# Transposes three tiles behind their scores instead of two, head 0's hash bits in a pair of score banks, and the identity loaded after head 0's queries

## The chip, the cores and the metric

The kernel runs on one core of a Trainium2 chip. The metric is device microseconds (us) for one launch, as the median of several runs. Below, PE is TensorE (matmuls), DVE is VectorE, ACT is ScalarE, POOL is GpSimd and SP is SyncE, whose queue issues nearly all transfers (DMAs). Times written as "at 16.19" are us from the start of the profiled execution.

## The reference

The program is hashed (LSH) attention followed by two layers of a gated feed-forward network. q, k and v have 2 batches, 8 heads, 768 positions and 64 channels, so there are 16 heads in all.

```python
q_bits = (einsum('bhsd,dk->bhsk', q, proj) > 0)   # 6 hash bits for each position
k_bits = (einsum('bhsd,dk->bhsk', k, proj) > 0)
mask   = bucket(q_bits)[:, :, :, None] == bucket(k_bits)[:, :, None, :]
scores = where(mask, q @ k.T / sqrt(D), -1e9)
attn   = exp(scores - max(scores));  attn = attn / (sum(attn) + 1e-9)
x = (attn @ v) laid out as (1536 rows, 512)
x = leaky(x @ w_in1) @ w_out1                     # 512 -> 2048 -> 512
x = (P(h) / (Q(h) + 1e-6)) @ w_out2, h = x @ w_in2   # 512 -> 2048 -> 512
```

## The kernel before

A head is worked in six tiles of 128 query rows. Each tile passes through four steps:

- **Scores** (`rows`, kinds `first`, `second`, `scores`): four PE matmuls of 384 columns write a pair of PSUM banks, two with the high parts of q and k (L559, from `qh` and `kx`) and two with the low parts (L564, from `ql` and `k2`). Twelve rows of `ql` and `k2` hold the hash bits, so that L564 also adds the mask's penalty.
- **Clamp** on DVE (L574) reads the pair of banks into an SBUF tile `x`, and **exp** on ACT (L580) works in place.
- **Transpose** (`flip`: "flip" and "turn" are the code's names): six PE matmuls of 128 columns with the identity `idf` (L606) write another pair of banks, named `t`. A copy, kind `take`, on ACT (L429) or DVE (L433), brings it to `pt`.
- When all six tiles of a head are copied, `mix` multiplies them by v: 24 PE matmuls (L649, `pv`) in two halves of 12.

Scores and transposes share three pairs of banks in turn (`bank_pair`, tag `s`). So a transpose has to wait until the clamp has emptied the pair used three turns before, and scores wait until a `take` has emptied theirs. `late` is the list of tiles whose transposes are still to come; `wait(2)` leaves two of them behind the scores.

For each head, `kT` and `qT` (128 x 768 floats, 0.393 MB each, tiles `rk` and `rq`) are loaded, and `k2`, `qh`, `kx` and `ql` are made from them. The hash bits come from PE matmuls against the projection (L480, tile `pb`). Head 0 and head 1 use their own `rk` and `rq`; from then on one set of matmuls serves two heads and has loads of its own, `kN` and `qN` (L472). For head 0, DVE writes the bits straight into `ql` and `k2` (`bits_at`, L489, four operations). For the others DVE writes a tile `bt` (L485), and four small DMAs (L496) carry its rows into `ql` and `k2`.

While PE is in attention, DVE and ACT also split the 64 weight blocks (`raw`, L319 and on) into high and low parts. After head 14 the matrix stages begin: 24 units of 96 PE matmuls of 512 columns (L679, L695, L698).

Every step is a task with durations per engine; `Plan.order` builds a list schedule from them, and the kernel issues its instructions in that order. `FAVOUR` gives each kind of task a bias to its rank and factors on its cost per engine. So a change of this table or of one task moves instructions everywhere.

Of the kernel before, what the change touches and what calls it, by code (L numbers as in the profile page):

```python
# [61 lines left out]
WARMUP = 9  # L62

PORT = ("dve", "pool")
FAVOUR = {
    "a_abs": (62.5, {}), "a_abs2": (202.2, {}), "a_exp": (-128.3, {"act": 0.17}), "a_g": (215.5, {}),
    "a_log": (1470.9, {"act": 0.52}), "a_mul": (-173.3, {"dve": 0.41, "pool": 0.47}), "a_n1": (584.8, {"dvp": 0.91}),
    "a_n2": (0, {"dvp": 0.84}), "a_p0": (-441.7, {"act": 3.65}), "a_p1": (240.4, {"act": 4.27}),
    "a_prep": (-94.8, {}), "a_quad": (-13, {"dvp": 0.98}), "a_sq": (89.8, {"act": 2.63}),
    "a_sum": (284.5, {"dve": 8.45, "pool": 0.09}), "awayb": (10.5, {}), "back": (-63.1, {"act": 0.05, "dvp": 0.04}),  # L70
    "backb": (672.3, {"act": 0.11, "dvp": 17.38}), "banks": (604.6, {"none": 1.11}), "bits": (205.6, {"pe": 2.45}),
    "bits0": (392.1, {"pe": 1.69}), "bits_at0": (-21.4, {}), "bits_at1": (-74.2, {}), "bits_at2": (-64.8, {}),
    "bits_at3": (-18.9, {}), "bits_ev": (-82.2, {"dvp": 0.3}), "bits_evb": (-222.6, {"dvp": 2.87}),
    "bits_mv": (310.2, {"dma": 2.11}), "bits_mvb": (5.8, {"dma": 0.57}), "bitsb": (-952.5, {"pe": 0.94}),
    "c_abs": (-16, {"act": 0.63}), "c_bits": (1.7, {"dve": 5.95}),
    "c_hi": (103.9, {"act": 0.14, "dve": 2.31, "pool": 23.21}), "c_lo": (1216.6, {"dve": 0.24}),
    "c_load": (18.4, {"dma": 0.12, "none": 3.41}), "c_prep": (-597.3, {"dve": 0.7}), "c_tail": (0, {"act": 0.38}),
    "clamp": (-286.8, {"dvp": 2.08}), "clampb": (35.5, {"dvp": 8.19}), "e_abs": (206.6, {"act": 2.31}),
    "e_bits": (-1934.6, {"dve": 0.36}), "e_lo": (-449.7, {"dve": 1.15}), "e_load": (147.1, {"dma": 0.27}),
    "e_out": (492.7, {}), "e_tail": (-99.1, {"act": 0.42}), "expo": (0, {"act": 0.67}),  # L80
    "expob": (-266, {"act": 1.51}), "eye": (239.2, {"dma": 2.17}), "f_abs": (-100.4, {"act": 1.32}),
    "f_bits": (-6, {}), "f_lo": (101.1, {"dve": 1.31}), "f_load": (819.2, {}), "f_out": (18.8, {}),
    "f_tail": (-511.9, {"act": 1.09}), "first": (239.8, {}), "flip": (4, {}), "flipb": (194, {"pe": 0.78}),
    "g_both": (-4.2, {}), "g_both0": (-3, {"dvp": 0.77}), "g_both1": (0, {"dvp": 0.39}),
    "g_hi": (-560.6, {"act": 0.68, "dvp": 47.43}), "g_hi0": (259, {"act": 5.33, "dvp": 1.56}),
    "g_hi1": (-238, {"act": 0.02, "dvp": 0.87}), "g_hi2": (-458.1, {"act": 0.14, "dvp": 0.3}), "g_lo": (142, {}),
# [6 lines left out]
    "load2b": (-81.7, {}), "loadb": (-131.6, {"dma": 2.11}), "o_add1": (-4732, {"dvp": 2.93}), "o_add2": (5.8, {}),
    "o_ev": (717.8, {"act": 1.21, "dvp": 0.02}), "o_ev0": (-19.1, {"act": 2.26, "dvp": 18.44}),
    "o_ev2": (632.5, {"act": 18.15, "dvp": 0.03}), "over": (-468.4, {"dvp": 0.04}), "overb": (271.3, {"dvp": 0.48}),
    "pv": (-688, {"pe": 1.11}), "pvb": (40.1, {}), "qh": (-33.7, {"act": 0.02, "dve": 0.44, "pool": 9.08}),
    "qh0": (-225.7, {"act": 1.4, "dve": 50.0, "pool": 0.11}),
# [5 lines left out]
    "scores": (-47.9, {"pe": 2.11}), "scores0": (-8.7, {}), "scoresb": (53.1, {}), "second": (-269.4, {}),
    "swap": (-61.6, {}), "take": (7.1, {"act": 0.02, "dvp": 50.0}), "takeb": (0, {"act": 0.02, "dvp": 0.11}),
    "u_abs": (100.6, {"act": 3.87}), "u_bits": (-317.8, {}), "u_hi": (14, {"act": 0.05, "dve": 0.58, "pool": 2.15}),
    "u_lo": (0, {"dve": 0.17}), "u_load": (-24.1, {"dma": 0.33}), "u_tail": (-125.7, {"act": 1.39}),
    "v_load": (-549.7, {"dma": 0.51}), "w_abs": (-207.7, {"act": 1.17}), "w_bits": (-597, {}),
    "w_hi": (435, {"act": 10.69, "dve": 19.85, "pool": 0.17}), "w_lo": (0, {"dve": 0.82}),
    "w_load": (0, {"dma": 2.6}), "w_tail": (-155.4, {"act": 12.89}), "warm": (-695.6, {}),
    "x_hi": (15.4, {"act": 3.32, "dve": 0.08, "pool": 0.74}),  # L110
    "x_hi2": (-2001.7, {"act": 0.23, "dve": 0.07, "pool": 50.0}), "x_lo": (296, {"dve": 0.07, "pool": 1.47}),
    "x_lo2": (-196.4, {"dve": 21.99, "pool": 10.09}), "zero": (247, {}),
# [158 lines left out]
def lsh_attention_moe_moe(ctx: ExitStack, tc: tile.TileContext, qT, kT, qN, kN, vN, consts, eye,  # L271
# [173 lines left out]
    def head(h):  # L445
# [57 lines left out]
        for n, src, r in (("rk", kT, R[0]), ("rq", qT, R[1])):  # L503
            plan.send("load" + z, load(n, src), 0.4, 1.0, (), [r])
# [13 lines left out]
        if h < 2 or h % 2 == 0:  # L518
            b = plan.buf("b")
            plan.add("bits" + z, bits_mm, {"pe": 0.98}, [*R, BZ], [b], cols=1536)  # L520
        if h:
# [4 lines left out]
            for n in range(2):
                plan.send("bits_mv" + z, move(n), 1.5, 0.22, [bt, *([B["kx"]] * n)], [B[("ql", "k2")[n]]], begin=NEAR)
        else:
            B["at"] = [Buf() for n in range(4)]
# [511 lines left out]
```

## Time and profile before

| what | value |
|---|---|
| median of 3 runs | 757.69 us (756.81 to 758.21) |
| time of the profiled execution | 757.42 us |
| its span, first to last instruction | 755.6 us |
| PE busy | 744.4 us (99%), mean granted clock 0.997 |
| DVE, ACT, POOL busy | 664.4, 513.3, 146.2 us |
| chain that ended last, by engine | PE 93%, DMA 4%, DVE 2%, issue 1% |

The profiled execution's own time is its span and 1.8 us around it. A busy PE is a PE with a matmul in flight; it can still be slow, when its clock is granted at half (1.2 instead of 2.4 GHz).

### The profile page before, as it was taken

To read this page: it belongs to the slowest core of one execution; us is meant where nothing else is said; L and a number is where in the kernel's file an instruction comes from. 1 tells how busy PE (TensorE), PEld (TensorE's weight loads), DVE (VectorE), ACT (ScalarE), POOL (GpSimd) and SP (SyncE) were. 2 spreads that over 40 slices of the span, in tenths; PEclk is the share of its full clock that TensorE was granted. 3 is DMA by queue.
4 is the path that set the end of the run, shared out by engine and by line. 5 is a ranking of instruction groups with operands and counts; after the bars stand their busy time and mean duration, and the time that the engine had idled before them with its cause. 6 is when DMAs were issued, how large, how long until landed. Compare 5 with 4: busy or idle time off the path is not lost.

```text
span 755.6 us, 10816 instructions
## 1 busy us (share of the span) xinstructions
PE 744.4 (99%) x3729; PEld 587.2 (78%) x3729; DVE 664.4 (88%) x1187; ACT 513.3 (68%) x881; POOL 146.2 (19%) x130
## 2 busy tenths in 40 slices
PE   7999999999999999999999999999999999999998
PEld 4677667676777888888888888888888888888886
DVE  6998999999989999998999899999898877778882
ACT  5889989978874654544454356887887686766660
POOL 4322211010000000000000000125533344433430
PEclk9999999999999999999999999999999999999999
DMA  6854666556332123256433652520202200200012
GB/s 231 238 172 132 184 181 162 175 189 190 121 109 67 72 96 112 100 179 194 139 108 117 208 173 93 195 112 1 111 1 112 111 1 1 111 1 1 14 57 97
DMA packets 36199, 88.21 MB, mean 117 GB/s; under 512 B 8800, under 2 KB 11952, under 8 KB 34608
## 3 DMA queue, kind: packets, MB, share of 16 engines
q1 hardware_dynamic: 35856, 87.35, 35.7%
q8 instruction: 29, 0.48, 0.2%
q14 instruction: 26, 0.21, 0.1%
q10 hardware_dynamic: 288, 0.17, 0.1%
HBM read 70.62 MB, written 15.78 MB: 114 GB/s over the span
## 4 chain that ended last, share of the span: by engine, by line
PE 93%; DMA 4%; DVE 2%; issue 1%; SPq 0%; POOL 0%; ACT 0%; DVEq 0%; ACTq 0%; POOLq 0%
PE h L679 35%; PE o L698 17%; PE o L695 16%; PE pv L649 8%; PE t L606 7%; PE s L559 4%; PE s L564 4%; DMA rq<-qT 2%; PE h L695 1%; DMA rq<-qN 1%; PE pb L480 1%; DVE x L574 1%; DVE acc L655 0%; DMA k<-bt 0%; DVE kx L466 0%
## 5 line engine op out<-in xcount | busy, mean ns | idle before, releaser
L679 PE MATMUL h<-xh,wih 128*128 128x512 f32 x384 | 150.2, 391 | 0.0
L679 PE MATMUL h<-xl,wih 128*128 128x512 f32 x384 | 149.8, 390 | 0.0
L679 PE MATMUL h<-xh,wil 128*128 128x512 f32 x384 | 149.4, 389 | 0.0
L574 DVE TENSOR_SCALAR_CACHE_REDUCE x<-s 128x768 f32<-128x768 f32 x96 | 90.8, 953 | 7.3 <-PE s L564 6.2
L580 ACT ACTIVATE x<-x,st 128x768 f32<-128x768 f32 x96 | 89.3, 931 | 8.3 <-DVE x L574 4.9
L606 PEld LDWEIGHTS t<-idf,x 128*128 128x128 f32 x576 | 65.8, 141 | 24.3 <-issue 8.5
L429 ACT ACTIVATE pt<-t 128x768 f32<-128x768 f32 x91 | 73.0, 806 | 16.8 <-PE t L606 16.5
L679 PEld LDWEIGHTS h<-xl,wih 128*128 128x128 f32 x384 | 72.1, 188 | 15.5
L679 PEld LDWEIGHTS h<-xh,wil 128*128 128x128 f32 x384 | 72.1, 188 | 15.2
L679 PEld LDWEIGHTS h<-xh,wih 128*128 128x128 f32 x384 | 72.1, 188 | 14.9
L606 PE MATMUL t<-idf,x 128*128 128x128 f32 x576 | 80.7, 277 | 2.8 <-ACT x L580 1.9
L744 POOL TENSOR_TENSOR x<-x,ap 128x512 f32<-128x512 f32 x48 | 62.5, 1303 | 100.6 <-ACT x L732 63.9
L698 PE MATMUL o<-woh,gl 128*128 128x512 f32 x192 | 74.9, 390 | 0.0
L698 PE MATMUL o<-woh,gh 128*128 128x512 f32 x192 | 74.8, 390 | 0.0
L698 PE MATMUL o<-wol,gh 128*128 128x512 f32 x192 | 74.8, 390 | 0.0
L649 PE MATMUL pv<-pt,vr 128*64 128x384 f32 x384 | 68.8, 494 | 0.0
L695 PE MATMUL o<-gh,wol 128*128 128x512 f32 x176 | 68.6, 390 | 0.0
L695 PE MATMUL o<-gh,woh 128*128 128x512 f32 x176 | 68.6, 390 | 0.0
L695 PE MATMUL o<-gl,woh 128*128 128x512 f32 x176 | 68.5, 389 | 0.0
L438 DVE TENSOR_TENSOR gl<-h,gh 128x512 fp32r<-128x512 f32 x96 | 64.8, 684 | 2.3 <-ACT gh L429 1.6
L429 ACT ACTIVATE gh<-h 128x512 fp32r<-128x512 f32 x72 | 43.0, 601 | 28.6 <-DVE h L718 16.9
L329 ACT ACTIVATE raw<-raw 128x512 uint32<-128x512 uint32 x64 | 43.0, 672 | 25.9 <-DMA raw<-w_out 12.9
(97 smaller groups left out, 1449.3 us busy)
## 6 DMA issues: line engine op xcount, KB each, us to landing
raw<-w_in SPq DMA_DIRECT2D x32, 512.0 KB
raw<-w_out SPq DMA_DIRECT2D x32, 512.0 KB
rk<-kT SPq DMA_DIRECT2D x16, 384.0 KB
rq<-qT SPq DMA_DIRECT2D x16, 384.0 KB
sp<-mag SPq DMA_DIRECT2D x24, 256.0 KB
sp<-w SPq DMA_DIRECT2D x16, 256.0 KB
vr<-vN SPq DMA_DIRECT2D x8, 384.0 KB
rs<-rd SPq DMA_DIRECT2D x32, 96.0 KB
```

The costliest lines, as they stand in the source:

```text
L329: s_.activation(self.low, self.low, AF.Copy, scale=2.0 ** -9 * (1 - 2.0 ** -22))
L429: s_.activation(out, in_, AF.Copy, scale=scale)
L438: eng[e].tensor_tensor(out, a, b, op=ALU.subtract)
L559: te.matmul(sp[:, j, :HALF], K["qh"][:, q], K["kx"][:, j * HALF:(j + 1) * HALF], start=True, stop=False)
L574: v_.tensor_scalar(x.rearrange("p (j c) -> p j c", j=2), T["s"][:, :, :HALF], SCALE, FAR, op0=ALU.mult, op1=ALU.min, accum_out=T["st"])
L580: s_.activation(T["x"], T["x"], AF.Exp, bias=T["st"], scale=-1.0, accum_out=tr["ss"][:, half, tt:tt + 1])
L606: te.transpose(o[:, c], T["x"][:, c], idf)
L649: te.matmul(T["pv"][64 * half:64 * half + 64, :HALF], tv["vr"][:, m, kt, :], E[half][0]["pt"][:, kt, :], start=(kt == 0), stop=(kt == NT - 1))
L679: te.matmul(hp, wt[:, kc, f], xt[:, kc], start=(n == 0), stop=(n == 3 * KC - 1))
L695: te.matmul(op, lt[:, m, d], rt, start=(n == 0), stop=(n == 3 * FT - 1))
L698: te.matmul(op, lt[:, d], rt[:, m], start=(n == 0), stop=(n == 3 * FT - 1))
L744: eng[e].tensor_tensor(P[a], P[a], P[b], op=op)
```

## The change

Four edits, and a new `FAVOUR` table:

```diff
-        if h < 2 or h % 2 == 0:
+        if h == 0:
+            b = plan.buf("s")
+            plan.add("bits0", bits0_mm, {"pe": 0.98}, [*R, BZ], [b], cols=1536)
+        elif h == 1 or h % 2 == 0:
             b = plan.buf("b")
...
+        def bits0_mm(e):
+            T["b"] = bank_pair("pb0")
+            for j in range(2):
+                for n, r in enumerate(("rq", "rk")):
+                    te.matmul(T["b"][64 * n:64 * n + 32, j, :HALF], Z[n], T[r][:, j * HALF:(j + 1) * HALF],
+                              start=True, stop=True)
...
         def bits_at(n):
-            to, j, r = T["ql" if n < 2 else "k2"], n % 2, slice(32 * n, 32 * n + 2 * NB)
-            v_.tensor_scalar(to[64:64 + 2 * NB, j * HALF:(j + 1) * HALF], P["b"][r, :HALF],
-                             cst[r, 0:1], cst[r, 1:2], op0=ALU.is_ge, op1=ALU.mult)
+            r = slice(64 * n, 64 * n + 2 * NB)
+            v_.tensor_scalar(T["k2" if n else "ql"][64:64 + 2 * NB].rearrange("p (j c) -> p j c", j=2),
+                             T["b"][r, :, :HALF], cst[r, 0:1], cst[r, 1:2], op0=ALU.is_ge, op1=ALU.mult)
...
-            for n in range(4):
+            for n in range(2):
...
+                if t == 2:
+                    w = plan.add("again", again, {"pe": 0.2267 * AGAIN}, [BR], [BPV], cols=512 * AGAIN)
+                    w.after([u])
...
+    EYE.follow(plan.tags["raw_qk"][1].writers[0])
...
-            wait(2)
-            if t == 1 and h:
+            wait(3)
+            if t == 2 and h:
                 finish(*todo)
...
-    "kxb": (-433.4, {"dve": 8.17}), "load": (14.8, {"dma": 8.2}), "load0": (1.8, {}), "load2": (-302.2, {}),
+    "load0": (15.9, {}), "load2": (220.2, {}), "load2b": (-539.2, {}), "loadb": (62.2, {"dma": 2.11}),
```

(The last two lines are one of each version of the table; nearly all its entries are changed.) The transposes now stand three tiles behind the scores, and `mix` of the head before is planned a tile later. Head 0's hash bits fill a pair of score banks, queries in rows 0 to 31 and keys in rows 64 to 95, and DVE writes them with two operations of 768 columns. `again` repeats eight matmuls of zeros, as at the start (`warm`), behind the scores of tile 2 of head 0. The identity's load is planned behind the load of head 0's `rq`.

How the order moves at the start on SP, the queue of the loads. `rk` and `rq` from `kT` and `qT` are head 0's, those from `kN` and `qN` are for the hash bits of heads 2 and 3, `idf` is the identity, `raw` weight blocks, `vr` values. Before:

```order
L844 DMA idf<-eye 128x128
L462 DMA rk_131<-kT 128x768
L462 DMA rq_143<-qT 128x768
L319 DMA raw<-w_in 128x512 x2
L472 DMA rk_149<-kN 128x768
L472 DMA rq_151<-qN 128x768
L540 DMA vr_155<-vN 128x768
```

and now:

```order
L474 DMA rk_130<-kN 128x768
L474 DMA rq_132<-qN 128x768
L464 DMA rk_144<-kT 128x768
L464 DMA rq_146<-qT 128x768
L866 DMA idf<-eye 128x128
L321 DMA raw<-w_in 128x512 x2
L553 DMA vr_155<-vN 128x768
```

The identity went behind head 0's queries, and the two loads for heads 2 and 3 went ahead of head 0's own.

On PE at the start, after the first nine `warm` matmuls, from the first scores (`s_0` to `s_3` are tiles 0 to 3 of head 0, `t_0` and `t_1` their transposes). Before:

```order
L559 MATMUL s_0_175<-kx_164,qh_171 128x384 x2
L559 MATMUL s_1_181<-kx_164,qh_171 128x384 x2
L559 MATMUL s_2_186<-kx_164,qh_171 128x384 x2
L564 MATMUL s_0_175<-k_162,ql_107 128x384 x2
L564 MATMUL s_1_181<-k_162,ql_107 128x384 x2
L564 MATMUL s_2_186<-k_162,ql_107 128x384 x2
L606 MATMUL t_0_214<-idf,x_0_202 128x128 x6
L559 MATMUL s_3_223<-kx_164,qh_171 128x384 x2
L564 MATMUL s_3_223<-k_162,ql_107 128x384 x2
L606 MATMUL t_1_234<-idf,x_1_205 128x128 x6
L480 MATMUL pb_250<-rq_192,zq 32x384 x2
```

and now:

```order
L572 MATMUL s_0_174<-kx_164,qh_171 128x384 x2
L572 MATMUL s_1_179<-kx_164,qh_171 128x384 x2
L577 MATMUL s_0_174<-k_162,ql_107 128x384 x2
L577 MATMUL s_1_179<-k_162,ql_107 128x384 x2
L572 MATMUL s_2_199<-kx_164,qh_171 128x384 x2
L577 MATMUL s_2_199<-k_162,ql_107 128x384 x2
L852 MATMUL warm<-rt 128x512 x8
L572 MATMUL s_3_223<-kx_164,qh_171 128x384 x2
L577 MATMUL s_3_223<-k_162,ql_107 128x384 x2
L482 MATMUL pb_231<-rq_185,zq 32x384 x2
L482 MATMUL pb_231<-rk_177,zk 32x384 x2
L622 MATMUL t_0_241<-idf,x_0_196 128x128 x6
```

The hash bits of head 1 (`pb_250`, now `pb_231`) stood behind the transposes of tiles 0 and 1; now they stand ahead of both, and the eight `warm` matmuls ahead of tile 3's scores. After them the order was: scores 4, transpose 2, bits of heads 2 and 3, scores 5, transpose 3, then head 1: scores 0, transposes 4, scores 1, transpose 5, scores 2, transpose 0, scores 3, half of `pv`, bits of heads 4 and 5. Now it is: scores 4, transpose 1, bits of heads 2 and 3, scores 5, transpose 2, then head 1: scores 0, transpose 3, scores 1, transpose 4, scores 2, transpose 5, bits of heads 4 and 5, scores 3, transpose 0, scores 4, transpose 1, half of `pv`.

On ACT in head 10 (`x_2` to `x_5` are exps, `pt<-t` the copies behind the transposes, `qh<-rq` makes a later head's `qh`). Before:

```order
L580 ACTIVATE x_2_1839,ss_0_1804<-x_2_1839,st_2_1840 128x768
L429 ACTIVATE pt_0_1849<-t_1_1854 128x6x128
L580 ACTIVATE x_3_1869,ss_0_1804<-x_3_1869,st_3_1870 128x768
L580 ACTIVATE x_4_1880,ss_0_1804<-x_4_1880,st_4_1881 128x768
L429 ACTIVATE pt_0_1849<-t_2_1891 128x6x128
L429 ACTIVATE qh_1914<-rq_1851 128x768
L429 ACTIVATE pt_3_1928<-t_3_1907 128x6x128
```

and now:

```order
L593 ACTIVATE x_3_1860,ss_0_1777<-x_3_1860,st_3_1861 128x768
L593 ACTIVATE x_4_1872,ss_0_1777<-x_4_1872,st_4_1873 128x768
L431 ACTIVATE pt_0_1865<-t_1_1878 128x6x128
L431 ACTIVATE pt_0_1865<-t_2_1893 128x6x128
L593 ACTIVATE x_5_1900,ss_0_1777<-x_5_1900,st_5_1901 128x768
L327 ACTIVATE mag<-raw 128x512
L331 ACTIVATE raw<-raw 128x512
L431 ACTIVATE pt_3_1947<-t_3_1930 128x6x128
```

The conversion `qh<-rq`, which needs a load to have landed, is gone from ACT's queue there. Over the whole kernel ACT makes 9 of the `qh` and `k` copies where it made 13, and none after head 10 where it made one in each head; POOL makes 21 where it made 16. DVE makes one `take` where it made five.

## Rows read from the trace of the kernel before

**Rows 1.** Stretches: us, busy us and instructions by engine, granted clock, DMA share, GB/s.
```profile
4.00:6.00 2.00, 1.65 (x4) 0.74 (x3) 0.81 (x1) 0.84 (x1) 0.00 (x0) 1.00 0.99 287
8.00:10.00 2.00, 1.00 (x6) 0.70 (x6) 1.94 (x4) 0.94 (x2) 0.86 (x1) 1.00 1.00 391
14.00:16.00 2.00, 2.00 (x9) 1.58 (x7) 1.52 (x3) 1.33 (x3) 0.70 (x1) 0.50 0.16 60
400.00:500.00 100.00, 100.00 (x441) 82.59 (x440) 91.51 (x167) 58.37 (x100) 8.44 (x6) 1.00 0.44 148
```

**Rows 2.** Timeline of the first 17 us: start, us, instruction, idle before it and its releaser.
```profile
1.45 4.21 PE L833 MATMUL warm<-rt 128*128 128x512 f32 x9 [1.45 <-DVE rt L858]
...
4.25 0.84 ACT L429 ACTIVATE k<-rk 128x768 fp32r<-128x768 f32 x1 [1.19 <-DMA rk<-kT]
...
6.09 0.85 PE L480 MATMUL pb<-rq,zq 128*32 128x384 f32 x2 [0.43 <-DMA rq<-qT]
...
7.48 0.69 DVE L489 TENSOR_SCALAR k<-pb,every 12x384 fp32r<-12x384 f32 x1 [1.27 <-PE pb L480]
...
9.69 1.28 PE L564 MATMUL s<-k,ql 128*128 128x384 f32 x6 [1.00 <-DVE k L489]
...
12.85 0.88 PE L606 MATMUL t<-idf,x 128*128 128x128 f32 x6 [1.88 <-ACT x L580]
...
16.19 0.86 PE L480 MATMUL pb<-rq,zq 128*32 128x384 f32 x2
```

**Rows 3.** Timeline from head 1's hash bits to those of heads 4 and 5.
```profile
17.48 0.62 PE L559 MATMUL s<-kx,qh 128*128 128x384 f32 x2
...
22.89 0.44 PE L564 MATMUL s<-k,ql 128*128 128x384 f32 x1 [0.29 <-DMA k<-bt]
...
23.11 0.43 SPq L472 DMA_DIRECT2D rq<-qN  x1
...
30.50 0.52 PE L480 MATMUL pb<-rq,zq 128*32 128x384 f32 x2 [0.29 <-DMA rq<-qN]
...
31.29 0.87 PE L606 MATMUL t<-idf,x 128*128 128x128 f32 x6
```

**Rows 4.** Timeline of PE in heads 4 to 6, where it waits for nothing.
```profile
83.91 0.60 PE L559 MATMUL s<-kx,qh 128*128 128x384 f32 x2
...
84.79 2.16 PE L649 MATMUL pv<-pt,vr 128*64 128x384 f32 x12
...
86.88 0.88 PE L606 MATMUL t<-idf,x 128*128 128x128 f32 x6
...
87.51 0.59 PE L559 MATMUL s<-kx,qh 128*128 128x384 f32 x2
...
88.29 0.82 PE L606 MATMUL t<-idf,x 128*128 128x128 f32 x6
...
88.86 0.60 PE L559 MATMUL s<-kx,qh 128*128 128x384 f32 x2
...
103.44 0.82 PE L606 MATMUL t<-idf,x 128*128 128x128 f32 x6
...
104.19 2.16 PE L649 MATMUL pv<-pt,vr 128*64 128x384 f32 x12
```

**Rows 5.** Timeline around PE's later waits, heads 11 to 13.
```profile
153.94 0.84 ACT L429 ACTIVATE qh<-rq 128x768 fp32r<-128x768 f32 x1 [1.02 <-DMA rq<-qT]
...
161.91 0.95 DVE L433 COPY pt<-t 128x768 f32<-128x768 f32 x1
...
162.91 0.61 PE L559 MATMUL s<-kx,qh 128*128 128x384 f32 x2 [0.34 <-DVE pt L433]
...
184.89 0.82 PE L606 MATMUL t<-idf,x 128*128 128x128 f32 x6
...
186.05 0.62 PE L559 MATMUL s<-kx,qh 128*128 128x384 f32 x2 [0.34 <-ACT pt L429]
...
187.58 0.88 PE L606 MATMUL t<-idf,x 128*128 128x128 f32 x6 [0.56 <-DVE x L574]
```

More of the change, by code (lines that the diff above doesn't have):

```diff
@@ L62 @@
 WARMUP = 9
+AGAIN = 8
 PORT = ("dve", "pool")
 FAVOUR = {
[L66 to L86, printed above, removed]
@@ L93 @@
[L93 to L97, printed above, removed]
@@ L103 @@
[L103 to L112, printed above, removed]
+    "a_abs": (35.5, {}), "a_abs2": (21, {}), "a_exp": (81.3, {"act": 0.17}), "a_g": (33.4, {}),
@@ new lines @@
+    "a_log": (49.4, {"act": 0.52}), "a_mul": (191.2, {"dve": 50.0, "pool": 0.58}), "a_n1": (0, {"dvp": 0.91}),
+    "a_n2": (684.5, {"dvp": 0.84}), "a_p0": (82.4, {"act": 3.65}), "a_p1": (1360.3, {"act": 4.27}),
+    "a_prep": (-35.1, {}), "a_quad": (-427.5, {"dvp": 0.98}), "a_sq": (754.6, {"act": 2.63}),
+    "a_sum": (-310.1, {"dve": 1.94, "pool": 0.12}), "again": (-61.1, {}), "away": (-7.5, {}), "awayb": (590.6, {}),
+    "back": (-165, {"act": 0.11, "dvp": 0.1}), "backb": (-1.8, {"act": 0.06, "dvp": 12.89}),
@@ new lines @@
+    "banks": (134.3, {"none": 1.11}), "bits": (653.3, {"pe": 2.45}), "bits0": (0, {"pe": 1.69}),
+    "bits_at0": (519.7, {}), "bits_ev": (0, {"dvp": 0.3}), "bits_evb": (0, {"dvp": 2.87}),
+    "bits_mv": (358.5, {"dma": 2.11}), "bits_mvb": (178.1, {"dma": 0.57}), "bitsb": (-53.4, {"pe": 0.94}),
+    "c_abs": (6.8, {"act": 0.63}), "c_bits": (373.5, {"dve": 5.95}),
+    "c_hi": (380.2, {"act": 0.09, "dve": 0.28, "pool": 0.04}), "c_lo": (953.1, {"dve": 0.24}),
+    "c_load": (-206, {"dma": 0.12, "none": 3.41}), "c_prep": (-351.7, {"dve": 0.7}), "c_tail": (6.4, {"act": 0.38}),
@@ new lines @@
+    "clamp": (307.8, {"dvp": 2.08}), "clampb": (-49.2, {"dvp": 8.19}), "e_abs": (0.6, {"act": 2.31}),
+    "e_bits": (-1703.8, {"dve": 0.36}), "e_lo": (-46.2, {"dve": 1.15}), "e_load": (52.2, {"dma": 0.27}),
+    "e_out": (136.6, {}), "e_tail": (-453.8, {"act": 0.42}), "expo": (-17.1, {"act": 0.67}),
+    "expob": (16.8, {"act": 1.51}), "eye": (188.5, {"dma": 2.17}), "f_abs": (-187.4, {"act": 1.32}),
+    "f_bits": (110.7, {}), "f_lo": (-42.8, {"dve": 1.31}), "f_out": (173.9, {}), "f_tail": (-249.1, {"act": 1.09}),
@@ new lines @@
+    "first": (-56, {}), "flip": (-74.4, {}), "flipb": (-0.2, {"pe": 0.78}), "g_both": (-1331.9, {}),
+    "g_both0": (-910.3, {"dvp": 0.77}), "g_both1": (831.9, {"dvp": 0.39}), "g_hi": (327.8, {"act": 0.03}),
+    "g_hi0": (-5.9, {"act": 48.81, "dvp": 29.81}), "g_hi1": (-23.5, {"act": 4.82, "dvp": 50.0}),
+    "g_hi2": (646.6, {"act": 0.37, "dvp": 2.79}), "g_lo": (117.2, {}), "g_lo0": (-5.3, {"dvp": 0.28}),
+    "g_lo1": (87.7, {"dvp": 1.07}), "g_lo2": (-531.1, {"dvp": 0.85}), "g_neg": (325.7, {"act": 1.54}),
@@ new lines @@
+    "ql0": (99.7, {"dve": 3.4, "pool": 17.96}), "qlb": (-2460.3, {"dve": 0.55, "pool": 18.33}),
+    "recip": (0, {"dve": 2.0}), "recipb": (-212.2, {"dve": 0.51}), "reload": (-54.2, {"dma": 0.45}),
+    "s1": (211.7, {"pe": 0.73}), "s10": (108.9, {}), "s11": (5.1, {"pe": 1.31}), "s12": (444, {}),
+    "s2": (15.4, {"pe": 5.53}), "s20": (-1299.1, {"pe": 2.84}), "s21": (35.9, {"pe": 0.75}), "s22": (83.5, {}),
+    "scores": (150.9, {"pe": 2.11}), "scores0": (-489.9, {}), "scoresb": (235.4, {}), "second": (-31.1, {}),
@@ new lines @@
+    "store": (-97.8, {}), "swap": (57.2, {}), "take": (272.2, {"act": 4.77, "dvp": 4.62}),
+    "takeb": (-32.2, {"act": 0.73, "dvp": 1.7}), "u_abs": (-150.9, {"act": 3.87}), "u_bits": (-294, {}),
+    "u_hi": (149, {"act": 0.02, "dve": 1.44, "pool": 4.34}), "u_lo": (112.2, {"dve": 0.17}),
+    "u_load": (869.4, {"dma": 0.33}), "u_tail": (73.7, {"act": 1.39}), "v_load": (-578.1, {"dma": 0.51}),
+    "w_abs": (782.1, {"act": 1.17}), "w_bits": (-507.1, {}),
+    "w_hi": (-1.7, {"act": 45.67, "dve": 0.45, "pool": 2.65}), "w_lo": (603.3, {"dve": 0.82}),
@@ L503, in head @@
         for n, src, r in (("rk", kT, R[0]), ("rq", qT, R[1])):
-            plan.send("load" + z, load(n, src), 0.4, 1.0, (), [r])
+            plan.send("load" + z, load(n, src), 0.4, 1.6 if h == 0 and n == "rq" else 1.0, (), [r])
         plan.add("k2" + z, lambda e: put(e, new("k2"), T["rk"]), COPY, [R[0]], [B["k2"]])
@@ L528, in head @@
         else:
-            B["at"] = [Buf() for n in range(4)]
-            for n in range(4):
-                plan.add(f"bits_at{n}", lambda e, n=n: bits_at(n), {"dvp": 0.7}, [b, *([B["kx"]] * (n > 1))], [B["at"][n]])
+            B["at"] = [Buf() for n in range(2)]
+            for n in range(2):
+                plan.add(f"bits_at{n}", lambda e, n=n: bits_at(n), {"dvp": 0.88}, [b, *([B["kx"]] * n)], [B["at"][n]])
         return T, B
@@ L826, in split, with again @@
                  [bx], [bx])
+    PV = {}
     def warm(e, count=WARMUP):
-        o = tl(ps, "pv", [128, 512], F32, "warm")
+        if not PV:
+            PV["o"] = tl(ps, "pv", [128, 512], F32, "warm")
         for n in range(count):
-            te.matmul(o, rt[:, :128], rt, start=True, stop=True)
+            te.matmul(PV["o"], rt[:, :128], rt, start=True, stop=True)
+    def again(e):
+        warm(e, AGAIN)
     def consts_load(e):
```

35 lines of the change are left out of this document (20 added, 15 removed).

## The prediction

> **What bounds the kernel now.** The table by engine comes first: PE is busy for 99% of the span, so only PE's time can be gained, and it must be seen where PE is not at its best. The windows of 100 us come next: in the matrix stages a window shows PE busy for all of its 100.00 us with 441 matmuls of 512 columns, 0.227 us each, while DVE has 91.51 busy and ACT 58.37 [rows 1]. There an edit on another engine changes nothing until it makes PE wait. The losses lie in attention, so the timeline of PE is read there, for gaps and for rows that are slower than their kind.
>
> The start has most of them. The nine `warm` matmuls take 4.21 us, 0.47 each: twice 0.227, half the clock. Then PE waits for `rq`, whose arrival lets the bits begin at 6.09. It waits 1.00 for DVE's fourth `bits_at` (second scores at 9.69) and 1.88 for the exp (transpose at 12.85), and behind these waits the granted clock of 14 to 16 is 0.50 [rows 1, 2]. It was granted in full again by 17.48, after PE had run without a break from 12.85. After that come short waits for `k<-bt` and for the load of `qN`, 0.29 each, up to 30.50 [rows 3]. The later waits are few: heads 11 to 13 have one of 0.34 and losses of 0.59 and 0.75 [rows 5]. In between, PE goes from instruction to instruction without waiting [rows 4].
>
> So two things decide: when head 0's chain gets going, and what the third tile between scores and transposes spares later.
>
> **The loads.** kN and qN (0.393 MB each) go ahead of head 0's kT and qT, and the identity (0.066 MB) behind: 0.72 MB more in front of `rq`. At 0.287 MB per us, the rate of 4 to 6 us, that is 2.5 us; at 0.391, the rate of 8 to 10, it is 1.85 [rows 1]. `rk` landed at 4.25 and `rq` at 6.09, 1.84 us for 0.393 MB, by which it is 3.4 [rows 2]. I take 2.9, between the two slower ones, because the first transfers of the queue are those that ran slowly: `rq` is there at 9.0 instead of 6.09. No measured row shows these two loads at the head of the queue; 1.85 and 3.4 are the ends.
>
> The Trainium skill, "DMA: Bandwidth & Descriptors", section "Specifications", gives about 358 GB/s as the limit of HBM for one core; by it 0.72 MB would be 2.0 us instead of 2.9. The trace has a stretch above that (391) and one below (287), so the measured rates stand.
>
> **Head 0's chain behind `rq`.** Now it takes 3.6 us from the bits to the second scores (6.09 to 9.69). Two `bits_at` of 768 columns replace four of 384. One of 384 took 0.69, so one of 768 lies between 0.69 and 1.38; I take 0.95, DVE's copy of 768 columns from a pair of banks [rows 2, 5]. Two of these cost 1.9 where three of 0.69 stood ahead of the second scores or beside them; `ql` (768 columns too) and `qh` (0.84 as the ACT copy) stand on the path as now. I take 3.9 us, with 3.6 and 4.3 as the ends: second scores at 12.9 instead of 9.69.
>
> **PE from there to head 1's bits.** PE pauses from 5.66, the end of `warm`, to 9.0. Work at full clock costs, from start to start: a tile of scores 0.78 ahead of a transpose, a transpose 0.57 to 0.63 ahead of scores (0.6), half of `pv` 2.09 [rows 4]; the four matmuls of a pair of bits I price as a tile of scores. From 12.9 come 8 matmuls of scores (1.56), `again` (8 x 0.227 = 1.8), tile 3 (0.78) and head 1's bits (0.78). Full clock: the bits end at 17.8. Half clock: a matmul of 384 columns takes 0.35 (three quarters of 0.47); the 8 of scores end at 15.7, and if the clock comes back as far into this burst as it does now, some 3.6 of `again` go at 0.47 and 4.4 at 0.227; then tile 3 and the bits, which end at 20.0. Now they end at 17.48 [rows 3]. Head 1's loads, whose queue has the same bytes ahead of it, arrive as now, by 16.19 [rows 2].
>
> **From the bits to equal work.** Next are three transposes (two of head 0's before the bits of heads 2 and 3, one after), two tiles of scores and those bits: 4.15, so head 1's scores 0 begin at 22.0 or 24.2. Their second half needs rows moved by DMA from `bt`; now that ran 5.4 us after the bits (22.89 against 17.48 [rows 3]). Again 5.4: 23.2 or 25.4, finished 0.4 later. Three transposes and two tiles of scores take 3.36: 27.0 or 29.2. Then the bits of heads 4 and 5, which were behind the half of `pv` and now are ahead of it, need `qN`. Its load was issued 5.6 us after the bits (23.11) and landed 7.4 us later (30.50) [rows 3]. Now a `raw` load less stands in front: 0.43 less for the issue, and of the 2.1 MB between, 0.52 less, so 5.5 us. That gives 28.5 or 30.7, with PE waiting 1.5 us behind it: no transpose and no scores pass the bits in PE's order. Add the bits (0.78), scores 3 and transpose 0 (1.38), and 2.25 for the half of `pv`, which was done at 31.29 and still has to come here. Equal work is reached at 32.9 or 35.1, against 31.29: the start costs **1.6** at full clock and **3.8** with the fall. The rows don't say whether the clock falls in a pause of 3.3 us; I take the middle, **2.7**.
>
> The Trainium skill, "TensorE: Matmul & The Clock Gate", section "Why this matters for your kernels", warns of idle gaps between bursts, after which the clock goes back to half. It speaks against this change: by it the start costs 3.8, not 2.7, and the sum is 760.1. The half clock of 14 to 16 behind two short pauses agrees with the fall, not with how long a pause it takes.
>
> **PE's order later.** In the order of the whole kernel ten halves of `pv` stand behind a transpose instead of three. A transpose ahead of `pv` takes 0.75 instead of 0.57 (0.18 more), a tile of scores ahead of `pv` 0.88 instead of 0.78 (0.10 more) [rows 4]. Seven times the difference of 0.08 is **+0.6**.
>
> **What comes back.** A transpose that stands three tiles behind has a tile (1.4 us) more for clamp and exp; and ACT no longer makes `qh` after head 10, where it waited 1.02 for the load ahead of the copy at 153.94. DVE makes one copy of 0.95 behind transposes instead of five. These are what stood ahead of PE's later losses: 0.34, 0.59 and 0.75, in all **-1.7** [rows 5]. The ends are 0 (the third tile also holds its pair of banks a turn longer, so scores may wait instead) and 3.0 (all small losses of the same kind after 31.29, by my reading of PE's whole timeline).
>
> **Costed at nothing.** The identity is needed by the first transpose alone, which comes several us behind its load; if it came late, the price is its 0.066 MB, 0.2 us. POOL takes over work from DVE and ACT in the matrix stages, hidden by PE's 100.00 busy of 100 [rows 1]; without that cover each late block would show as a wait of PE there. The two `bits_at` fewer free DVE for under 1 us, already in the chain.
>
> **Sum.** The profiled execution took 757.42 (span 755.6 and 1.8 around it); the median of the runs is 757.69, 0.27 above it and within their spread. 757.42 + 2.7 + 0.6 - 1.7 = **759.0**, with its own range of 757.6 to 760.2. A difference under 0.2%, 1.5 us, can hardly be told from none here.
>
> **Rivals.**
> - **The loads cost little and the later waits go** (faster, 0.27). At 0.391 MB per us `rq` is there at 7.95, the chain keeps its 3.6, and the clock stays up: bits of head 1 end at 17.0 (their loads let them begin at 16.2), scores 0 are done at 22.8, 3.36 more give 26.2, and `qN` lands at about 26.3 (1.57 MB at 0.391). Equal work at 30.7: -0.6. With 2.4 given back: 757.42 - 0.6 + 0.6 - 2.4 = **755.0**. The rate of 8 to 10 us speaks for it; that of 4 to 6 against it.
> - **The clock falls in the longer pause** (slower, 0.22). PE goes into head 0 at half clock, the start costs 3.8, and the waits that go are half of those counted, 0.8: 757.42 + 3.8 + 0.6 - 0.8 = **761.0**. It decides once the second scores run at 0.35 per matmul up to `again`. For it: the fall behind the 1.88 wait; against it: after the 0.43 pause at 6.09 nothing fell, and the new pause is one, not two.
> - **The change doesn't do what it says** (0.13). Head 1's loads and the moves from `bt` hold PE at the start as now, so head 0's delay is hidden; and the waits of heads 11 to 13 go to other tiles. Only PE's order is left: 757.42 + 0.6 = **758.0**.
>
> **How the numbers follow.** The forecast has 0.38, since its terms are the middles of what the rows bound. Of its 0.38, 0.24 lie within 0.2%, 0.13 above and 0.01 below; the faster rival gives 0.25 to faster and 0.02 to same; the slower one 0.21 and 0.01; the last one 0.10 same, 0.02 faster, 0.01 slower. Together: faster 0.28, same 0.37, slower 0.35. The range takes in the faster rival down to 754.2 (all 3.0 given back) and the slower one with 0.6 above it, to 761.6 (no more than 0.2 given back).
>
> **What the changed profile would show.** The first bits begin near 9.0 behind `rq` (8.0 speaks for the faster rival), the second scores near 12.9. PEclk in the slices from 7 to 17 decides between 1.6 and 3.8. The bits of heads 4 and 5 wait about 1.5 behind `qN`. In heads 11 to 13 no row of PE waits for a `pt` or an `x`; if new waits for `pt<-t` stand ahead of scores, the third tile has only moved them. Work equal to that of 31.29 at 33 to 35 confirms the start; from there on, PE should be 1 us faster than before. I would be most wrong if the loads run at another rate, or if PE waits in the matrix stages.

## The result and the profile after

| what | before | changed |
|---|---|---|
| median | 757.25 us (4 runs) | 766.38 us (763.15 to 766.76, 4 runs) |
| ratio | | 1.0112, 95% interval 1.0095 to 1.0129 |
| profiled execution (span) | 757.42 (755.6) | 766.76 (765.0) |
| PE busy | 744.4 | 750.2 |

The change made the kernel slower by 1.1%, 9 us; the forecast was 759.0, in a range that ended at 761.6.

The start comes first. Here are windows of the changed kernel (us, busy us of PE, PEld, DVE, ACT and POOL with instructions, granted clock, DMA share, GB/s), to be held against [rows 1]:

```profile
6.00:8.00 2.00, 0.00 (x0) 0.00 (x0) 0.48 (x1) 0.00 (x0) 0.00 (x0) 1.00 1.03 386
8.00:10.00 2.00, 1.39 (x6) 0.76 (x8) 1.73 (x3) 0.89 (x2) 0.00 (x0) 1.00 0.99 397
16.00:18.00 2.00, 2.00 (x7) 1.71 (x6) 1.92 (x5) 2.00 (x5) 0.00 (x0) 1.00 0.00 0
```

The loads run at 386 and 397 GB/s; PE does nothing from 6 to 8. And PE's timeline, to be held against [rows 2, 3]; the `warm` at 16.54 is `again`:

```profile
1.45 4.21 PE L852 MATMUL warm<-rt 128*128 128x512 f32 x9 [1.45 <-DVE rt L880]
8.61 0.82 PE L490 MATMUL pb<-rq,zq 128*32 128x384 f32 x1 [2.95 <-DMA rq<-qT]
...
9.22 0.85 PE L490 MATMUL pb<-rq,zq 128*32 128x384 f32 x1
...
11.41 1.65 PE L572 MATMUL s<-kx,qh 128*128 128x384 f32 x4
13.84 1.62 PE L577 MATMUL s<-k,ql 128*128 128x384 f32 x4 [0.78 <-DVE k L499]
...
16.54 2.64 PE L852 MATMUL warm<-rt 128*128 128x512 f32 x8
19.01 0.51 PE L572 MATMUL s<-kx,qh 128*128 128x384 f32 x2
...
20.59 0.87 PE L622 MATMUL t<-idf,x 128*128 128x128 f32 x6
...
32.10 0.52 PE L482 MATMUL pb<-rq,zq 128*32 128x384 f32 x2 [1.54 <-DMA rq<-qN]
...
37.87 0.62 PE L572 MATMUL s<-kx,qh 128*128 128x384 f32 x2
```

The reader should see four things. PE's pause after `warm` is 2.95 long, where it was 0.43. From 8.61 on, a pair of bits matmuls starts 0.61 to 0.64 after the pair ahead of it, twice the 0.32 of a run below; `again` takes 2.47 for eight matmuls where full speed makes 1.8, and only from 19.01 on are the scores as fast as anywhere: PE, which was at half speed in `warm`, comes out of its pause at half speed and stays there up to about 18. The second scores come at 13.84 (9.69 before). And the bits of heads 4 and 5 wait 1.54 for `qN`. Work equal to that done at 31.29 before is the start of 37.87 less one tile of scores and one transpose that are ahead in this order (1.53, from 34.26 to 35.79): 36.34. So the start costs **5.05**.

In the kernel before, `warm` is at half speed as well, but there the bits follow after 0.43 us, and PE is at full speed by the first scores: six matmuls in 1.31, where the changed kernel has four in 1.65 at 11.41.

```profile
7.37 1.31 PE L559 MATMUL s<-kx,qh 128*128 128x384 f32 x6
```

The start differs between executions. With the same loads in the same order, ACT starts on `rq` at 8.49 in this one and at 7.62 to 8.50 in the experiments below. In two of these whose start is unchanged (the second buffer for `bt`, and two `ql` on DVE), the row behind the first half of `pv` starts at 36.85 and 36.84, 1.0 earlier than here (37.87), so there the start costs 4.0.

PE's waits in the whole changed kernel, by what ended them (us in all, times, longest); the first and the last of these lines are of the start:

```profile
PE pb L490 <- DMA rq<-qT: 2.9, 1, 2.9
PE s L572 <- ACT pt L431: 2.3, 3, 1.0
PE t L622 <- DVE x L587: 1.6, 5, 0.5
PE pb L482 <- DMA rq<-qN: 1.5, 1, 1.5
```

Measured as losses (start to start, less what the same step takes without a wait), PE loses 6.1 us after 45 us and up to the end of attention, where the kernel before lost 3.1. Of the three losses of [rows 5] two are gone. The third is still there: counted in PE's order, the transpose that waits for `x` at 187.58 before and at 196.44 now is the same, the first of head 13, and it loses 0.6 where it lost 0.7. Other losses stand between 45 and 144. The largest two, with what is ahead of them, and that of 196.44:

```profile
39.57 1.83 POOL L440 TENSOR_TENSOR ql<-qh,rq 64x768 fp32r<-64x768 f32 x1
...
39.76 2.19 DVE L355 SCALAR_TENSOR_TENSOR wil<-mag,raw 128x512 fp32r<-128x512 uint32 x1
...
41.88 0.94 DVE L587 TENSOR_SCALAR_CACHE_REDUCE x<-s 128x768 f32<-128x768 f32 x1
...
45.91 0.79 ACT L431 ACTIVATE pt<-t 128x768 f32<-128x768 f32 x1
...
46.76 0.62 PE L572 MATMUL s<-kx,qh 128*128 128x384 f32 x2 [0.94 <-ACT pt L431]
...
126.92 1.53 SPq L506 DMA_DIRECT2D ql<-bt  x2
...
131.56 0.68 DVE L495 TENSOR_SCALAR bt<-pb,every 128x384 fp32r<-128x384 f32 x1 [1.64 <-DMA ql<-bt]
...
132.16 0.95 DVE L587 TENSOR_SCALAR_CACHE_REDUCE x<-s 128x768 f32<-128x768 f32 x1
...
133.20 0.94 ACT L593 ACTIVATE x<-x,st 128x768 f32<-128x768 f32 x1 [2.16 <-DVE x L587]
...
134.14 0.79 ACT L431 ACTIVATE pt<-t 128x768 f32<-128x768 f32 x1
...
135.07 0.59 PE L572 MATMUL s<-kx,qh 128*128 128x384 f32 x2 [1.03 <-ACT pt L431]
...
196.44 0.88 PE L622 MATMUL t<-idf,x 128*128 128x128 f32 x6 [0.43 <-DVE x L587]
```

At 39.76 a DVE instruction of the weights, 0.69 long in the three others of its kind in attention, takes 2.19 beside POOL's `ql`; the clamp behind it is late, ACT's exp after it, ACT's copy `pt` after that, and PE's scores lose 1.2. At 131.56 DVE has stood 1.64, because `bt` could not be written again before the move `ql<-bt` had read it; a clamp stands behind, and the chain clamp, exp, copy, scores loses PE 2.05 in all between 133.2 and 138.9.

Together: 5.05 + (6.1 - 3.1 = 3.0) + 1.3 for PE's order = 9.35, against 766.76 - 757.42 = 9.34. The 1.3 is what is left, and most of it lies in the matrix stages. From 238.78 the kernel before has 2,256 matmuls of 512 columns ahead of it and needs 516.9 us to the end of the span; the changed kernel has 2,220 from 255.47 and needs 509.5. The 36 fewer are worth 8.2 us (0.227 each), and only 7.35 are saved: the matrix stages take 0.8 longer, though PE waits nowhere in them. Traces of experiments below that keep this plan have the same 509.5; why it is so, no run shows. The other 0.5 is order within attention, where 0.6 was forecast for halves of `pv`; the last heads now also have 84 of the 512-column matmuls between their tiles, in seven bursts, before it was 48 in four.

### The profile page after: what moved, and what is told of

Its sections match the earlier page's. It is cut to its first block, busy times and chain, and to the rows that moved or that the text cites. A ratio compares the mean times of both kernels' runs of the same rounds, so it can differ in the third digit from the quotient of the medians.

```text
span 765.0 us, 10795 instructions
## 1 busy us (share of the span) xinstructions
PE 750.2 (98%) x3737; PEld 591.0 (77%) x3737; DVE 638.1 (83%) x1139; ACT 531.5 (69%) x912; POOL 164.9 (22%) x145
## 4 chain that ended last, share of the span: by engine, by line
PE 89%; DVE 4%; DMA 3%; ACT 2%; issue 1%; SPq 0%; POOL 0%; DVEq 0%; POOLq 0%; ACTq 0%
PE h L695 34%; PE o L714 17%; PE o L711 16%; PE pv L665 6%; PE t L622 6%; PE s L572 3%; PE s L577 3%; DVE x L587 2%; DMA rq<-qT 2%; PE h L711 1%; ACT x L593 1%; DMA rq<-qN 1%; PE pb L482 1%; DMA rd<-ss 1%; DVE kx L468 1%
## 5 line engine op out<-in xcount | busy, mean ns | idle before, releaser
L760 POOL TENSOR_TENSOR ap<-ap,t 128x512 f32<-128x512 f32 x48 | 63.7, 1326 | 121.6 <-ACT t L763 101.5
L431 ACT ACTIVATE pt<-t 128x768 f32<-128x768 f32 x95 | 75.7, 806 | 16.3 <-PE t L622 15.4
L431 ACT ACTIVATE gh<-h 128x512 fp32r<-128x512 f32 x92 | 55.3, 602 | 45.6 <-DVE h L775 22.9
L818 DVE TENSOR_TENSOR acc<-acc,o 128x512 f32<-128x512 f32 (+1 forms) x73 | 49.3, 676 | 24.3 <-PE o L714 19.6
```

Of the source, the lines that this page charges most:

```text
L431: s_.activation(out, in_, AF.Copy, scale=scale)
L760: eng[e].tensor_tensor(P[a], P[a], P[b], op=op)
L818: v_.tensor_tensor(a, a, o, op=ALU.subtract if moe else ALU.add)
```

## Experiments

Times are medians of the runs beside runs of the kernel before on the same chip (756.8 to 757.1 there). Edits work on the list `order`, after the plan is made, so all other instructions keep their places; only two runs (marked) plan anew. The ratio of each run to the kernel before is uncertain by 1 to 2 us, as that of the changed kernel is, so a difference of less than about 2 us between two runs is not shown by their times; there the trace has to decide.

**Head 0's loads first.**

```diff
     order = plan.order()
+    early = [t for t in order if t.kind == "load0"]
+    order = early + [t for t in order if t.kind != "load0"]
```

> The changed kernel with one edit: on SP the loads of head 0's kT and qT are issued ahead of kN and qN; every other engine keeps its order. Theory 1 (the two loads put ahead delay head 0, and with the clock still at half they cost some 5 us at the start; PE's waits of heads 2 to 13, 6.1 us against 3.1 before, come from the new table by itself): rq lands near 6.0 instead of 8.6, second scores near 10 instead of 13.84, equal work 4 us earlier, 762.4 in all. Theory 2 (besides, the late start puts the engines out of step with the order that was planned for them, so POOL and DVE get in each other's way later): 3 us of the later waits go as well, 759.4. Rival 3 (head 1's loads hold PE anyway): no more than 1 us is gained, 765.

Measured: 762.67 (1.0079, 1.0066 to 1.0093), 3.7 less than the changed kernel; the two intervals don't overlap. PE's timeline of this run:

```profile
5.41 0.48 PE L490 MATMUL pb<-rq,zq 128*32 128x384 f32 x1
...
5.73 0.48 PE L490 MATMUL pb<-rq,zq 128*32 128x384 f32 x1
...
9.76 0.94 PE L577 MATMUL s<-k,ql 128*128 128x384 f32 x4 [1.88 <-DVE k L499]
...
32.79 0.62 PE L572 MATMUL s<-kx,qh 128*128 128x384 f32 x2
...
41.67 0.62 PE L572 MATMUL s<-kx,qh 128*128 128x384 f32 x2 [0.94 <-ACT pt L431]
...
130.47 0.59 PE L572 MATMUL s<-kx,qh 128*128 128x384 f32 x2 [1.03 <-ACT pt L431]
```

The bits begin at 5.41, without a pause behind `warm`, and at full speed (0.32 from pair to pair). The second scores are at 9.76. Equal work is at 32.79 - 1.52 = 31.27, so the start costs nothing against 31.29, though `again` is still in it. Between the profiled executions the gain is 4.6: the start is 5.1 earlier, and 0.5 comes back ahead of the matrix stages. The waits of 46.76 and 135.07 are at 41.67 and 130.47, equally long, 5.1 and 4.6 earlier. Theory 1 holds; theory 2, that lateness puts the engines out of step, fails: the waits belong to the order. At full speed the chain from the first bits to the second scores takes 4.35 here (4.07 in the next run), where it took 3.60 with four operations.

**PE kept busy until the loads land.**

```diff
-        for n in range(count):
+        for n in range(22 if count == WARMUP else count):
```

> The changed kernel with 22 matmuls of zeros at the start instead of 9, so that PE is busy until about 8.5, when head 0's rq lands; nothing else moved. It leaves the loads late and takes away only PE's pause of 2.95. If the half clock of 8.6 to 18 is the larger part of what the start costs: bits and first scores take half as long, second scores at 12.5 instead of 13.84, again and tile 3 end at 16.5 instead of 19.8, equal work 2 to 3 us earlier: 763 to 764. Rival: the chain on DVE and ACT behind rq and head 1's loads set the pace and the clock hardly matters: 765.5 to 766.5.

Measured: 767.7 (762.95 to 769.2). PE's timeline:

```profile
1.45 6.69 PE L852 MATMUL warm<-rt 128*128 128x512 f32 x22 [1.45 <-DVE rt L880]
8.26 0.48 PE L490 MATMUL pb<-rq,zq 128*32 128x384 f32 x1
...
8.58 0.48 PE L490 MATMUL pb<-rq,zq 128*32 128x384 f32 x1
...
12.33 0.93 PE L577 MATMUL s<-k,ql 128*128 128x384 f32 x4 [1.59 <-DVE k L499]
...
34.74 0.62 PE L572 MATMUL s<-kx,qh 128*128 128x384 f32 x2
...
183.01 0.68 DVE L495 TENSOR_SCALAR bt<-pb,every 128x384 fp32r<-128x384 f32 x1 [3.43 <-DMA rs<-rd]
```

The loads are late here too (ACT starts on `rq` at 8.14, in the changed kernel at 8.49), but the bits go from pair to pair in 0.32, and equal work is reached at 34.74 - 1.54 = 33.2: 3.1 earlier than in the changed kernel's profiled execution. Held against the run with two `ql` on DVE, where `rq` was there at 8.05, it is 2.1 earlier. So **half speed costs 2.1, with `rq` there at the same time, and the lateness of the loads 1.9**; the other 1.0 of the 5.05 is what the profiled execution lost beyond those with the same start.

The median doesn't show it. In the profiled execution DVE stood 3.43 at 183.01, which the changed kernel's execution did not, and PE's losses behind the start are 5.7 more than there. The row names a load `rs`, but the instruction doesn't touch `rs`: it writes `bt`, and the move out of `bt` that it has to wait for is the likelier cause, as at 131.56; the trace doesn't settle it. Of the six times two are at 763 to 764, as forecast, and four at 766.7 to 769.2; whether this wait parts them is not shown. The forecast of the start held, that of the median did not.

**Without `again`.** The eight matmuls are left out of the issue.

> The changed kernel without the eight repeated matmuls of zeros (again); nothing else moved. If they are only work in PE's way: 1.8 to 2.5 us less at the start, of which head 1's loads, there at about 16, and the load of qN behind which PE waits 1.5 may take back 1.5; time 764 to 766. If they are what lifts PE out of half clock: tile 3, the bits and transposes run at half clock instead, about 2 us more, and the time stays at 766 or goes up.

Measured: 765.49 (1.0108, 1.0092 to 1.0124), 0.9 less, which the intervals don't tell from none. In its trace the bits of head 1 start at 17.55 and run at full speed (0.34 from pair to pair), so the speed comes back without them too: they are work in PE's way. The bits of heads 4 and 5 come 2.2 earlier (29.87; `rq` came 0.35 earlier in this execution), but PE's waits for `x` and `pt` rise from 3.9 to 5.0.

**A second buffer for `bt`.**

```diff
-            P["bt"] = tl(hp, "bt", [128, HALF], F32R, f"bt{h}")
+            P["bt"] = rt[:, :HALF] if h // 2 % 2 else tl(hp, "bt", [128, HALF], F32R, f"bt{h}")
```

> The changed kernel with a second buffer for bt (every other one lies in the tile of zeros, which is free after the start); orders as in the changed kernel. In it DVE stood 1.64 at 131.56, waiting to overwrite bt until the move ql<-bt had read it, with two clamps queued behind. If that wait makes PE's losses from 133.2 to 138.9 (1.3 + 0.35 + 0.4 and the waits around, some 2.3 in all): they go, 764. Rival: ACT's and DVE's queues are too full there anyway and the same losses appear a tile later: 766, no change.

Measured: 763.93 (1.0089, 1.0074 to 1.0105), 2.45 less; its interval still overlaps that of the changed kernel. In its timeline DVE writes the bits (now into `rt`) without a wait, and PE's rows from 130 on follow each other at 0.57 and 0.78:

```profile
128.76 0.68 DVE L495 TENSOR_SCALAR rt<-pb,every 128x384 fp32r<-128x384 f32 x1
...
132.02 0.82 PE L622 MATMUL t<-idf,x 128*128 128x128 f32 x6
...
132.59 0.59 PE L572 MATMUL s<-kx,qh 128*128 128x384 f32 x2
```

The wait for `bt` is shown as the cause of the 2.05 lost there. It is not the whole difference between the two profiled executions (2.8): PE's losses behind the start are 1.8 lower in all, and the start itself is 1.0 shorter, where `rq` came 0.9 earlier.

**`ql` off POOL.** All of them on DVE, then only the two beside the stretched DVE instructions (`t.eng = "dve"` for these tasks).

> The changed kernel with all ql subtractions (64x768) on DVE, where six were on POOL (1.82 us each, beside which single DVE instructions took 2.19 instead of 0.69 at 39.76 and 2.03 instead of 1.02 at 81.31). Theory 2, contention of POOL and DVE: those two stretches go, PE's waits at 46.76 (0.94) and 87.60 (0.35) go with them, 1.5 to 2.5 us less: 764. Rival: DVE has six times 0.95 more to do and is what the transposes wait for, so nothing is gained or 1 to 2 us are lost: 766 to 768.

> The changed kernel with two of POOL's ql subtractions on DVE: those of 39.57 and 80.69, beside which one DVE instruction each took 2.19 and 2.03. If POOL's instruction makes DVE's long, and that the waits behind: the loss of 1.2 at 46.76 and 1.7 between 81 and 89 go, 763.5 to 764.5. If only the first goes: 765. Rival, as with all ql on DVE: no gain, 766 to 767.

Measured: 767.08 (1.0135, 1.0115 to 1.0155) with all, 765.24 (1.0096, 1.0080 to 1.0113) with two; neither is told from the changed kernel by its time. With two, DVE's instruction is short again and the wait of 46.76 is gone (0.2 of the 1.2 lost there stays):

```profile
38.73 0.69 DVE L355 SCALAR_TENSOR_TENSOR wil<-mag,raw 128x512 fp32r<-128x512 uint32 x1
...
40.21 0.94 DVE L440 TENSOR_TENSOR ql<-qh,rq 64x768 fp32r<-64x768 f32 x1
...
44.77 0.62 PE L572 MATMUL s<-kx,qh 128*128 128x384 f32 x2
```

The losses of 81 to 89 fell from 1.3 to 0.9 only, and one at 193 grew from 0.6 to 1.2. With all on DVE new losses came at 45.35 (0.36), 59.88 (0.44) and 98.73 (0.33). So POOL's instruction does make DVE's long and PE wait; that is worth 1.0 at this place, less in all (0.7 over attention), and with all on DVE PE's losses over attention rise by 1.0. The Trainium skill, "SBUF — State Buffer", section "Who interferes with whom", says that a DVE instruction with two inputs in SBUF contends with a GpSimd instruction that reads SBUF, and that the order of issue decides who blocks; the trace agrees: POOL's `ql` starts first, at 39.57, and ends at 41.40, and the 2.19 end 0.55 later.

**The third tile.** In the kernel before alone (planned anew), taken out of the changed kernel (planned anew), and taken out on PE alone: each of 72 transposes goes ahead of the scores that it stood behind, all other engines' orders kept.

```diff
# the kernel before
-            wait(2)
-            if t == 1 and h:
+            wait(3)
+            if t == 2 and h:
# the changed kernel, PE alone
+    for f in [t for t in pe if t.kind in ("flip", "flipb")][6:13 * NT]:
+        i = pe.index(f)
+        j = next(j for j in range(i - 1, -1, -1) if pe[j].kind in ("scores", "scoresb"))
...
+            pe.remove(f)
+            pe.insert(j, f)
```

> The kernel before with one edit: transposes three tiles behind the scores and mix a tile later; its old table, loads, bits and identity stay (its order is planned anew). If the third tile by itself gives slack: the 3.1 us of later waits shrink to about 1, 755 to 756. If the third tile holds a pair of banks a turn longer and costs as many waits as it spares, or a table that was not made for it makes new ones: 757 to 762. The start should stay as before, second scores at about 9.7.

> The changed kernel with two tiles behind the scores and mix a tile earlier, as before, under the new table (the order is planned anew); loads, bits pair, again and identity as changed. If the third tile makes the later waits: they fall back to about 3 and only the start's 5 us stay, 762. If the new table needs the third tile as the old one needed two (798 with three): far slower, 775 or more.

> The changed kernel with 72 transposes (from head 1's first to head 12's last) each ahead of the tile of scores that it stood behind, so that PE has them two tiles behind the scores again; ACT, DVE, POOL and SP keep their orders word for word. This tests the third tile alone, without a new plan. If the third tile is what lets transposes run without waiting for exps: waits for x and losses appear in every head, 0.3 us or more for each transpose that comes early, 775 and up. If it gives nothing, since scores wait for copies (pt) three turns of the banks later with either depth: 765 to 768, and the 6 us of later waits keep their places.

Measured: 798.08, 779.02 and 798.33. PE's waits in the first of them, the largest two:

```profile
PE h L679 <- DVE gl L438: 13.3, 6, 6.8
PE s L559 <- ACT pt L429: 4.5, 5, 1.7
```

The largest is in the matrix stages, where no transpose stands at all: a plan under a table that was set for another program. In the third run the scores wait for copies 23 times, 19.3 us in all (none of these for longer than 2.2), for instance:

```profile
66.73 0.94 ACT L593 ACTIVATE x<-x,st 128x768 f32<-128x768 f32 x1 [1.10 <-DVE x L587]
...
67.66 0.79 ACT L431 ACTIVATE pt<-t 128x768 f32<-128x768 f32 x1
...
68.50 0.61 PE L572 MATMUL s<-kx,qh 128*128 128x384 f32 x2 [0.83 <-ACT pt L431]
```

ACT's queue has the exp ahead of the copy, and the exp waits for the clamp of scores that now come later; with the third tile they come in time. Each table fits its own depth, and the other queues are written for it. These runs don't say what a third tile is worth under a table made for it; that stays open. Nor does any run take the pair of banks for the bits, or the identity's new place, by itself.

**Together.** Loads first, no `again`, second `bt`, two `ql` on DVE, and the bits of heads 4 and 5 behind the first half of `pv`; then also one `raw` load ahead of a move; then that with transposes at two tiles.

> The changed kernel with five edits of its issue order: head 0's loads first (4 to 5 us by the run with that alone), no again (0.9 by its run), bt in two buffers (2.3 if the wait of DVE is the cause), the bits of heads 4 and 5 behind the first half of pv as in the kernel before (the wait of 1.96 behind qN), and the two ql subtractions that ran on POOL beside stretched DVE instructions (39.76 and 81.31) on DVE (1.5). If the losses are separate and each of them has the cause named: 766.4 - 4.3 - 0.9 - 2.3 - 1.5 - 1.5 = 756, level with the kernel before. If the third tile itself keeps PE waiting for copies (pt) in other places: 759 to 761.

> The five edits of the combination, and one raw load of head 2 ahead of the move ql<-bt in SP's queue: in the combination ACT stood 2.16 at 38.98 for that load, and PE 2.23 at 41.86 for a copy queued behind it on ACT. If that is the cause: 1.4 us less than 758.8, 757.4. Rival: the move comes late instead and holds the scores: 758.8 or more.

> The same with the 72 transposes two tiles behind the scores. If the third tile is worth something once the other losses are gone, it is slower than the run beside it by more than 2 us; if not, it is within 1 us of it, 757 to 758.5.

Measured: 758.84 (1.0028, 1.0014 to 1.0042), 759.21 and 795.73. The first gives back 7.5 of the 9, but it is still slower than before by 0.3%, of which the 0.8 us of the matrix stages are untouched. ACT's and PE's rows in it:

```profile
38.98 0.68 ACT L327 ACTIVATE mag<-raw 128x512 f32<-128x512 f32 x1 [2.16 <-DMA raw<-w_in]
...
41.02 0.79 ACT L431 ACTIVATE pt<-t 128x768 f32<-128x768 f32 x1
...
41.86 0.61 PE L572 MATMUL s<-kx,qh 128*128 128x384 f32 x2 [2.23 <-ACT pt L431]
```

A weight load lands late, `mag` waits 2.16 for it on ACT, an exp and the copy queue behind, and PE stands 2.2. The run with a `raw` load sent earlier shows the same wait:

```profile
33.09 0.38 SPq L321 DMA_DIRECT2D raw<-w_in  x1
...
34.83 0.53 SPq L321 DMA_DIRECT2D raw<-w_in  x1
...
39.23 0.69 ACT L327 ACTIVATE mag<-raw 128x512 f32<-128x512 f32 x1 [2.06 <-DMA raw<-w_in]
```

It does not test the cause, because it moved the other load. By the semaphore that `mag` waits for, ACT needs the load issued at 33.09 (32.73 in the run without the move), and its last part landed at 39.20 (38.95). The load that was moved is the next one, issued at 34.83 instead of 36.17; it landed at 41.85, behind `mag`'s start. Why the needed one takes 6 us to land, and what sending it earlier would give, stays open. The run with transposes at two tiles is 36 us slower, as the one above: queues written for three tiles don't fit two. No version ran faster than the kernel before.

## Why the prediction was wrong

- **Bounds and places.** That PE alone counts held. That the matrix stages neither give nor take held for waits, not for time: they cost 0.8, which the sum has at nothing.
- **Loads and chain.** `rq` was forecast at 9.0; the bits could start on it at 8.61, and ACT at 7.6 to 8.5 in all executions with this order. The loads ran near the upper of the rates (386 and 397 GB/s). Two `bits_at` took 1.07 each (0.95 forecast), and the chain behind `rq`, 3.9 in the forecast, took 4.07 and 4.35 at full speed and 5.23 here.
- **"I take the middle, 2.7"** is the first step that failed. The start cost 5.05 (4.0 in two other executions), above even the half-clock end of 3.8. A fall of the clock was treated as an open case and averaged with its absence. But nothing had to fall: the prediction's own row has `warm` at 0.47 per matmul, half speed, in both kernels. Before, the bits followed 0.43 later, at first still at half speed (0.61 from 6.09 to 6.70), and PE was at full speed by 7.37; so that "nothing fell" after this pause was no sign that a pause is harmless. Now PE stood for 2.95 and went on at half speed. And in the half-clock case only the work behind the second scores was priced. The bits (0.61 from pair to pair, where full speed is 0.32) and the first scores were at half speed as well, so the second scores came at 13.84, not 12.9; `again` took 2.5, not the 1.8 of full clock or the 2.7 of the mix; and 0.5 more went behind an `x` at 28.32. The sentence on the Trainium skill's "TensorE: Matmul & The Clock Gate" stood on the right side: a pause between bursts and half speed behind it, which the run with 22 matmuls shows as 2.1 to 3.1 us. The page tells of a clock that goes back to half; here it had not yet risen.
- **"What comes back", -1.7,** is the second, and the larger: +3.0 was measured. Two of the three waits named did go, as forecast; the third, for `x` in head 13, stayed (0.6 of 0.7), though its transpose has a tile more of time. The step assumed that a new order makes no new ones and that waits come from load waits on ACT. The new ones come from queues that the forecast costed at nothing: DVE behind a DMA (`bt`, 2.05 by its trace), and POOL beside DVE (1.0 at its largest place).
- **PE's order, +0.6,** had the right sign: 0.5 is left for it in the balance, beside the 0.8 of the matrix stages.
- **Rivals.** The slower one came nearest in mechanism (half speed from the first scores on; it was from the bits on) and had the wrong size: 761.0, since it too let waits go. The faster one needed a clock that stays up, and it was still at half; its rate for the loads was the better one (`rq` at 7.95).

## What to carry to other kernels

At a cold start, count what PE does between its first matmuls and the first data: two loads sent ahead of the needed ones cost 1.9 in lateness and 2.1 to 3.1 in speed, since PE paused while it was still at half speed. A new order of queues is no saving of waits: each in-order queue where an instruction can wait for a DMA or another engine, with a clamp or copy behind it, has to be walked through, and a table of priorities is worth only as much as the program that it was set for (22 and 41 us above the kernel before, where the depth of one met the table of the other).

## What the runs showed of the hardware

The granted clock of the windows doesn't show half speed at the start: from 8 to 18 it reads 1.00, while matmuls start twice as far apart as at full speed (0.61 to 0.64 for a pair of bits, 0.32 in other runs). It is the other way round in the run with PE's transposes at two tiles, whose windows read 0.95 from 20 us up to the end, and yet hold as many matmuls of 512 columns as any (442 in this one):

```profile
300.00:400.00 100.00, 100.00 (x442) 82.63 (x441) 91.85 (x165) 55.93 (x97) 1.75 (x2) 0.95 0.42 135
```

But the 0.95 is not without meaning there: a half of `pv` takes 2.17 from start to start in that run and 2.09 in the changed kernel. The distance from one start to the next tells the speed of a shape more safely than that column. And loads vary: the same two loads ahead of the same `rq` let ACT start on it at 7.62 in one execution and at 8.50 in another.
